# Turning the rows of the second part by transposing DMAs instead of by TensorE

## The chip, the cores and the metric

One core of a Trainium2 chip runs the whole program. The time is device time of one execution, in microseconds (us); before the change it is 3302.31 us, the median of three runs (3301.95 to 3308.06). Engines: PE is TensorE, DVE is VectorE, ACT is ScalarE, POOL is GpSimd, SP is SyncE, which here only issues DMAs. Each has its own instruction queue and works in order; a wait holds up all that stands behind it on that engine.

## The reference

Three steps, one after the other, on 8 x 3072 = 24576 rows of 256 numbers:

```python
X = fft(fft(x, axis=1), axis=2).real              # rows of 256
do = x @ w_skip > 0                               # only these rows meet an expert
e = argmax(x @ w_gate); g = softmax(x @ w_gate)[e]
x[do] += g * (relu(x @ w1[e]) @ w2[e])            # 8 experts, 256 -> 1024 -> 256
h = x @ w_in                                      # 256 -> 2048
P = a0 + a1*h + a2*h**2 + a3*h**3
Q = 1 + |b0|*|h| + |b1|*h**2
out = (P / (Q + 1e-6)) @ w_out                    # 2048 -> 256
```

## The kernel before, in words

Every float32 number is carried as two float16 numbers, a high half (the rounded value) and a low half (what is left), and every product is three float16 matmuls: high by high, high by low, low by high.

The first part (to about 566 us) does the Fourier transforms, decides the route of each row, and scatters rows of 258 numbers (256 values, row number, gate weight) into a sorted list XS in HBM. Rows without an expert come to lie in tiles of 512, rows with one in batches of 256 of one expert.

The second part, which the change touches, works on 48 tiles of 512 rows. 22 come from XS straight (tile `xt`), 26 are made by the experts (tile `xf`), each from two of 52 batches (tile `xm`). It is one loop over 48 x 8 = 384 iterations `i`, each of which takes 256 of the 2048 columns of `h` of a tile. In an iteration, in written order:

- `z_mm1(i)`: 12 matmuls of 512 columns give `u` in PSUM. PE needs the rows turned: 128 of their 256 values on the partitions, row numbers along the free axis.
- `z_1(i)`: ACT makes T (L968) and Y (L969) from `u`; DVE makes T (L970) from T and `u`. `u` has two PSUM buffers, which the experts' first product uses too.
- `z_3(i-1)` (L978, ACT), `z_mm2(i-5)` (24 matmuls into `accz`), and after the last piece of a tile `z_end`: a copy by ACT (L1016) and four scatters by POOL (L1017).
- `z_hi(i-2)`: DVE's L988, gh from T and Y, both in SBUF.
- one step or none of the experts' list `all_moe`: half the first product of a batch, with its evacuation (L923, L924), the begin of the next batch (`moe_begin`), the other half, half the second product, its other half with L932, which adds the expert's rows to `xm`.
- `z_2(i)` (L974) and `z_4(i-1)` (L982) on ACT; `z_lo(i-3)`, DVE's L1000; `z_rest(i-2)`, DVE's L993 and then POOL's L994, which reads T and V and writes V. L1000 reads that V one iteration later.
- where `i % 8` is 3, `begin` of the next tile, and where it is 5, `begin_2`: they make that tile's turned halves, which are read from the next `i % 8 == 0` on.

So on DVE the order around a tile's begin is L988, (expert work), L1000, L993, (begin), L970, L988. POOL's L994 follows L993.

Turning a piece of 256 rows, before: `transpose_half` (L872 to L878) puts four 128x128 float32 blocks through PE against an identity (L876) into one PSUM bank, ACT copies it as the high half (L877), DVE subtracts that from the PSUM bank for the low half (L878). A tile takes two such pieces, half a tile at `i % 8 == 3` and half at 5; a batch takes one.

SP issues in written order: the loads of `xt` (two buffers), of `xm` (three) and of the expert's weights `mw` (2 MB, two buffers, waits for PE to be done with the batch before last), and the loads and stores that split the later experts' weights (L1034 to L1050).

Of the kernel before, what the change touches and what calls it, by code (L numbers as in the profile page):

```python
# [8 lines left out]
F32 = mybir.dt.float32  # L9
F16 = mybir.dt.float16  # L10
I32 = mybir.dt.int32
AF = mybir.ActivationFunctionType
ALU = mybir.AluOpType
AX = mybir.AxisListType
PSUM = bass.MemoryType.PSUM
SYNC = mybir.DependencyInfo(mybir.DependencyClass.Sync, mybir.DependencyReason.DATA)

B, SEQ, D = 8, 3072, 256
# [5 lines left out]
TILE = 512  # L24
# [8 lines left out]
HALF = 256  # L33
# [95 lines left out]
def program(tc, x, w_skip, w_gate, w1, w2, w_in, w_out, a, b, f1, cs, tw, tok, ut, small, lt8, slot, out):  # L129
    nc = tc.nc  # L130
    pe, act, dve, pool, sp = nc.tensor, nc.scalar, nc.vector, nc.gpsimd, nc.sync
    es = ExitStack()
    with es:
# [7 lines left out]
        ident = pers.tile([128, 128], F32, name="ident")  # L141
# [122 lines left out]
        rows = {}  # L264
# [323 lines left out]
        for r in range(R0):  # L588
            sp.dma_start(out=XS[SKIP0 + r * TILE:SKIP0 + (r + 1) * TILE, :].rearrange("(p r) c -> p r c", p=128),
                         in_=dum[:, None, :].to_broadcast([128, 4, ROW]))  # L590
# [48 lines left out]
        def pool_of(name, bufs, space=None):  # L639
            return fb.enter_context(tc.tile_pool(name=name, bufs=bufs, reuse_waits="tile", **({} if space is None else {"space": space})))  # L640

        wk = pool_of("wk", 1)
        xtp = pool_of("xtp", 2)
        xsp = pool_of("xsp", 2)
        ggp = pool_of("ggp", 4)
        elp = pool_of("elp", 4)
        hhp = pool_of("hhp", 2)
        xmp = pool_of("xmp", 3)
        xfp = pool_of("xfp", 2)
        pl = pool_of("pl", 1)  # L650
        pll = pool_of("pll", 1)
# [1 line left out]
        wsp = pool_of("wsp", 2)  # L653
        psh = pool_of("psh", 2, PSUM)
        psz = pool_of("psz", 1, PSUM)
        psm = pool_of("psm", 1, PSUM)

        wi = wk.tile([128, 4, 2, 1024], F16, name="wi")
        wo = wk.tile([128, 4, 2, 1024], F16, name="wo")
# [204 lines left out]
                if e % 2:  # L864
                    yield

        def split_pair(tag, n):
            th = xsp.tile([128, 2, n], F16, tag=tag + "h", name="th")
            tl = xsp.tile([128, 2, n], F16, tag=tag + "l", name="tl")
            return th, tl  # L870

        def transpose_half(src, th, tl, tag="mt"):  # L872
            u = psm.tile([128, 2, HALF], F32, tag=tag, name="ut")
            for h in range(2):
                for r in range(2):
                    pe.transpose(u[:, h, r * 128:r * 128 + 128], src[:, r, h * 128:h * 128 + 128], ident[:])  # L876
            act.activation(th, u[:], AF.Copy)  # L877
            dve.tensor_tensor(out=tl, in0=u[:], in1=th, op=ALU.subtract)  # L878

        def mm1(u, w, f0, nf, xh, xl):  # L880
            for s in range(nf):
                n = 0
                for k in range(2):
                    wh, wl = w(k, 0, f0 + s), w(k, 1, f0 + s)
                    for sta, mv in ((wh, xh), (wh, xl), (wl, xh)):
                        pe.matmul(u[:, s, :], lhsT=sta, rhs=mv[:, k, :], start=(n == 0), stop=(n == 5))  # L886
                        n += 1

        def mm2(acc, w, f0, nf, hh, hl, first, last):
# [9 lines left out]
        xf_of = {}  # L899

        def moe_begin(t):
            xh, xl = split_pair("m", HALF)
            transpose_half(t, xh[:], xl[:], "m")
            return xh, xl

        def moe_steps(t, w, xh, xl, xf, ids, k):

# [39 lines left out]
        Z = {}  # L947
        outs = []

        def z_begin(src, ids, n, k):  # L950
            if k == 0:
                Z[n] = dict(x=split_pair("z", TILE), ids=ids, src=src)
            xh, xl = Z[n]["x"]
            c = slice(k * HALF, k * HALF + HALF)
            transpose_half(Z[n]["src"][:, 2 * k:2 * k + 2], xh[:, :, c], xl[:, :, c])

        def z_mm1(i):
            n, j = divmod(i, 8)
            u = psh.tile([128, 2, TILE], F32, tag="h", name="u")
            mm1(u, wif, 2 * j, 2, *Z[n]["x"])  # L960
            T = elp.tile([128, 1024], F32, tag="T", name="T")
            V = elp.tile([128, 1024], F32, tag="V", name="V")
            Y = elp.tile([128, 1024], F32, tag="Y", bufs=5, name="Y")
            U[i] = dict(u=u[:].rearrange("p s n -> p (s n)"), T=T[:], V=V[:], Y=Y[:])

        def z_1(i):
            d = U[i]
            act.activation(d["T"], d["u"], AF.Square, scale=A[0], bias=A[1])  # L968
            act.activation(d["Y"], d["u"], AF.Abs, scale=A[4])  # L969
            dve.scalar_tensor_tensor(out=d["T"], in0=d["T"], scalar=A[2], in1=d["u"], op0=ALU.add, op1=ALU.mult)  # L970

        def z_2(i):
            d = U[i]
            act.activation(d["V"], d["Y"], AF.Square, bias=A[5])  # L974

        def z_3(i):
            d = U[i]
            act.activation(d["Y"], d["V"], AF.Ln, bias=A[6])  # L978

# [142 lines left out]
        def begin(n):  # L1122
            if n and not ready and cur["s_used"] == S2:
                while not ready:
                    next(moe)
            if ready:
                src, ids = ready.pop(0)
            else:
                s = cur["s_used"]
                src = xt.pop(("S", s))  # L1130
                ids = new_ids()
                dve.tensor_copy(out=ids[:], in_=src[:, :, D])
                cur["s_used"] += 1
            z_begin(src, ids, n, 0)

        def begin_2(n):
            z_begin(None, None, n, 1)
            feed()

        begin(0)  # L1140
# [43 lines left out]
        with tc.For_i(0, rem, 1) as it:  # L1184
            xf = xfp.tile([128, 4, D], F32, tag="xf", name="xf")
            ids = new_ids()
            for k in range(2):
                t = xmp.tile([128, 2, ROW], F32, tag="xm", name="xm")
                r = sp.value_load(plan[0:1, bass.ds(it * 2 + (C_LROW + k), 1)], min_val=0, max_val=NROWS - HALF)
                e = sp.value_load(plan[0:1, bass.ds(it * 2 + (C_LEXP + k), 1)], min_val=0, max_val=E - 1)  # L1190
                sp.dma_start(out=t[:], in_=rows_of(r, HALF))
                sp.dma_start(out=mw[k][:], in_=WD[bass.ds(e, 1)].rearrange("o p k h n -> p (o k) h n"))
                for _ in moe_steps(t, mw[k], *moe_begin(t), xf, ids, k):
                    pass
            n = NTILES
            for k in range(2):
                z_begin(xf, ids, n, k)
            for i in range(n * 8, n * 8 + 8):
                z_mm1(i)
                d = U[i]  # L1200
                act.activation(d["T"], d["u"], AF.Identity, scale=A[11], bias=A[10])
                act.activation(d["V"], d["u"], AF.Square)
                act.activation(d["Y"], d["u"], AF.Abs, scale=A[12])
                dve.tensor_tensor(out=d["T"], in0=d["T"], in1=d["u"], op=ALU.mult)
                dve.scalar_tensor_tensor(out=d["T"], in0=d["T"], scalar=A[9], in1=d["u"], op0=ALU.add, op1=ALU.mult)
                dve.scalar_tensor_tensor(out=d["V"], in0=d["V"], scalar=A[13], in1=d["Y"], op0=ALU.mult, op1=ALU.add)
                act.activation(d["Y"], d["V"], AF.Ln, bias=A[14])
                z_4(i)
                z_hi(i, 8)
                z_rest(i, 14)  # L1210
                z_lo(i, 8)
                z_mm2(i)
            z_end(n, False, 15)
# [27 lines left out]
```

## Time and profile before

| | |
|---|---|
| median of three runs | 3302.31 us |
| the profiled execution: its own time, its span | 3295.73 us, 3293.7 us |
| granted TensorE clock, mean | 0.959 |
| PE busy, share of the span | 3034.3 us, 92% |
| DVE | 2818.9 us, 86% |
| ACT | 2525.9 us, 77% |
| POOL | 1406.6 us, 43% |
| chain that ended last | PE 61%, DVE 20%, ACT 7%, issue 5% |
| L994, POOL, V from T and V, 128x1024 | 384 times, 2381 ns |
| L988, DVE, gh from T and Y, 128x1024 | 384 times, 2060 ns |
| L1000 and L993, DVE, 128x1024 | 384 times each, 1272 and 1275 ns |

Times of an instruction run from its start to its end; PE's matmuls and DVE's operations overlap their neighbours by a little, so sums are made from start to start. The share of busy time counts an operation that has started and waits for a resource as busy.

### The profile page before, as it was taken

What the parts mean: (1) busy time and instruction counts of PE and PEld (TensorE: products, weight loads), DVE (VectorE), ACT (ScalarE), POOL (GpSimd) and SP (SyncE); (2) the same over time, 40 slices, a digit from 0 to 9 for tenths busy, and PEclk for the clock granted to TensorE, in tenths of its full rate; (3) what the DMA queues carried; (4) which work ended last, traced back from release to release, by engine and by line L of the source; (5) the groups of instructions that cost most, each with busy time, mean ns of one, the idle gap of its engine ahead of it and who ended that gap; (6) DMA issues with size and microseconds to landing.
All of it is one profiled execution on the core that took longest, in us unless ns stands there. A gap on an engine that the chain in (4) does not pass through costs nothing.

```text
span 3293.7 us, 57696 instructions
## 1 busy us (share of the span) xinstructions
PE 3034.3 (92%) x23586; PEld 2214.6 (67%) x23586; DVE 2818.9 (86%) x2929; ACT 2525.9 (77%) x2694; POOL 1406.6 (43%) x796
## 2 busy tenths in 40 slices
PE   6678656799989999999999999999999999999996
PEld 5556444477767777776777777777777777777764
DVE  5667544899999999998899988999989999899986
ACT  5556442688878888888888888888888888888884
POOL 0445442454434444443444344444444444444444
PEclk8889877899999999999999999999999999999998
DMA  8344443131111112111211110011002000100000
GB/s 204 126 126 141 129 129 143 69 99 45 64 63 33 52 62 71 39 43 60 73 40 43 62 38 25 24 49 42 21 11 78 20 20 20 61 28 20 7 14 14
DMA packets 75617, 198.09 MB, mean 60 GB/s; under 512 B 12243, under 2 KB 36180, under 8 KB 72404
## 3 DMA queue, kind: packets, MB, share of 16 engines
q1 hardware_dynamic: 54612, 135.42, 13.7%
q0 software_dynamic: 18432, 50.55, 4.3%
q10 hardware_dynamic: 2304, 8.39, 0.6%
q8 instruction: 186, 3.05, 0.4%
q14 instruction: 83, 0.68, 0.1%
HBM read 190.69 MB, written 77.05 MB: 81 GB/s over the span
## 4 chain that ended last, share of the span: by engine, by line
PE 61%; DVE 20%; ACT 7%; issue 5%; another core or an unknown queue 3%; DMA 3%; POOL 0%; ACTq 0%; SPq 0%; DVEq 0%; POOLq 0%
PE u L886 26%; PE accz L896 20%; PE acc L896 8%; DVE gh L988 6%; DVE T L970 4%; DVE V L993 3%; PE u L256 2%; DVE gl L1000 2%; DMA out<-ob,ids 1%; ACT Y L969 1%; PE ut L876 1%; ACT T L968 1%; DMA xt<-in_x 1%; PE u L241 1%
## 5 line engine op out<-in xcount | busy, mean ns | idle before, releaser
L994 POOL TENSOR_TENSOR V<-T,V 128x1024 f32<-128x1024 f32 x384 | 914.2, 2381 | 1428.5 <-DVE V L993 1331.5
L896 PE MATMUL accz<-wo,gh 128*128 128x256 f16 x6144 | 1034.8, 274 | 2.8 <-ACT ob L1016 2.8
L886 PE MATMUL u<-th,wi 128*128 128x512 f16 x3072 | 984.6, 382 | 39.8 <-DVE T L970 38.7
L896 PE MATMUL accz<-wo,gl 128*128 128x256 f16 x3072 | 840.9, 274 | 13.0 <-DVE gl L1000 10.7
L886 PEld LDWEIGHTS <-wi 128*128 128x128 f16 x4608 | 453.2, 98 | 515.5 <-issue 61.3
L988 DVE SCALAR_TENSOR_TENSOR gh<-T,co,Y 128x1024 f16<-128x1024 f32 x384 | 791.1, 2060 | 0.0
L896 PEld LDWEIGHTS <-gh 128*128 128x128 f16 x6144 | 603.7, 98 | 156.3 <-issue 3.9
L968 ACT ACTIVATE T<-u,co 128x1024 f32<-128x1024 f32 x384 | 462.8, 1205 | 289.3 <-PE u L886 257.7
L970 DVE SCALAR_TENSOR_TENSOR T<-T,co,u 128x1024 f32<-128x1024 f32 x384 | 488.9, 1273 | 129.8 <-ACT Y L969 123.4
L886 PE MATMUL u<-tl,wi 128*128 128x512 f16 x1536 | 586.6, 382 | 0.1
L1000 DVE SCALAR_TENSOR_TENSOR gl<-V,co,Y 128x1024 f16<-128x1024 f32 x384 | 488.6, 1272 | 41.6 <-POOL V L994 41.6
L993 DVE SCALAR_TENSOR_TENSOR V<-V,co,gh 128x1024 f32<-128x1024 f32 x384 | 489.6, 1275 | 0.0
L978 ACT ACTIVATE Y<-V,co 128x1024 f32<-128x1024 f32 x384 | 442.8, 1153 | 0.0
L974 ACT ACTIVATE V<-Y,co 128x1024 f32<-128x1024 f32 x384 | 440.7, 1148 | 0.5 <-DVE gl L1000 0.4
L969 ACT ACTIVATE Y<-u,co 128x1024 f32<-128x1024 f32 x384 | 427.4, 1113 | 0.0
L982 ACT ACTIVATE Y<-Y 128x1024 f32<-128x1024 f32 x384 | 404.6, 1054 | 0.0
L896 PEld LDWEIGHTS <-gl 128*128 128x128 f16 x3072 | 301.8, 98 | 52.0 <-DVE gl L1000 13.5
L886 PE MATMUL u<-th,mw 128*128 128x256 f16 x1664 | 292.7, 274 | 7.7 <-DVE T L970 5.2
L1017 POOL DMA_INDIRECT out<-ob,ids x192 | 245.8, 1280 | 77.2 <-issue 44.2
L896 PE MATMUL acc<-mw,hh 128*128 128x256 f16 x1664 | 278.1, 273 | 0.0
L886 PEld LDWEIGHTS <-mw 128*128 128x128 f16 x2496 | 245.8, 98 | 39.7 <-issue 9.8
L886 PE MATMUL u<-tl,mw 128*128 128x256 f16 x832 | 228.3, 274 | 1.3 <-DVE tl L878 1.3
(206 smaller groups left out, 3456.0 us busy)
## 6 DMA issues: line engine op xcount, KB each, us to landing
mw<-wd SPq DMA_DIRECT2D x50, 2048.0 KB
xt<-in_x SPq DMA_DIRECT2D x64, 384.0 KB
xm<-xs SPq DMA_DIRECT2D x52, 258.0 KB
wf<-in_moe_w SPq DMA_DIRECT2D x48, 256.0 KB
wd<-ws SPq DMA_DIRECT2D x48, 256.0 KB
xt<-xs SPq DMA_DIRECT2D x22, 516.0 KB
wd<-ws ACTq DMA_DIRECT2D x16, 512.0 KB
wr<-in_moe_w_in SPq DMA_DIRECT2D x4, 1024.0 KB
```

The source lines that it names most:

```text
L886: pe.matmul(u[:, s, :], lhsT=sta, rhs=mv[:, k, :], start=(n == 0), stop=(n == 5))
L896: pe.matmul(acc[:, r, :], lhsT=sta[:, c], rhs=mv, start=(first and r % 2 == 0 and s == 0 and n == 0), stop=(last and s == nf - 1 and n == ...
L968: act.activation(d["T"], d["u"], AF.Square, scale=A[0], bias=A[1])
L969: act.activation(d["Y"], d["u"], AF.Abs, scale=A[4])
L970: dve.scalar_tensor_tensor(out=d["T"], in0=d["T"], scalar=A[2], in1=d["u"], op0=ALU.add, op1=ALU.mult)
L974: act.activation(d["V"], d["Y"], AF.Square, bias=A[5])
L978: act.activation(d["Y"], d["V"], AF.Ln, bias=A[6])
L982: act.activation(d["Y"], d["Y"], AF.Exp, scale=-1.0)
L988: dve.scalar_tensor_tensor(out=h[:], in0=d["T"], scalar=A[a0], in1=d["Y"], op0=ALU.add, op1=ALU.mult)
L993: dve.scalar_tensor_tensor(out=d["V"], in0=d["V"], scalar=A[c], in1=h[:], op0=ALU.add, op1=ALU.mult)
L994: pool.tensor_tensor(out=d["V"], in0=d["T"], in1=d["V"], op=ALU.subtract)
L1000: dve.scalar_tensor_tensor(out=l[:], in0=d["V"], scalar=A[a0], in1=d["Y"], op0=ALU.add, op1=ALU.mult)
```

## The change

The rows are split before they are turned. ACT copies them as float16 (high half), DVE subtracts (low half), both into a tile `rows` in SBUF, and one transposing DMA, issued by SP, turns both halves, 16 blocks of 128x128 for a tile and 8 for a batch. A tile is now begun in one piece, at `i % 8 == 3`. PE's identity transposes and their PSUM bank go; the experts' second product gets two PSUM banks. The turned tile has another order, so a matmul's moving operand is four runs of 128 columns (two for a batch) where it was one of 512 (256). To make room, `xm` has two buffers for three and Y four for five.

```diff
+        rsp = pool_of("rsp", 1)
-        xmp = pool_of("xmp", 3)
+        xmp = pool_of("xmp", 2)
-        psm = pool_of("psm", 1, PSUM)
+        psm = pool_of("psm", 2, PSUM)
...
-        def transpose_half(src, th, tl, tag="mt"):
-            u = psm.tile([128, 2, HALF], F32, tag=tag, name="ut")
-            for h in range(2):
-                for r in range(2):
-                    pe.transpose(u[:, h, r * 128:r * 128 + 128], src[:, r, h * 128:h * 128 + 128], ident[:])
-            act.activation(th, u[:], AF.Copy)
-            dve.tensor_tensor(out=tl, in0=u[:], in1=th, op=ALU.subtract)
+        def split_turned(src, nr, tag):
+
+            rows = rsp.tile([128, 2, nr, D], F16, tag=tag, name="rows")
+            act.activation(rows[:, 0], src, AF.Copy)
+            dve.tensor_tensor(out=rows[:, 1], in0=src, in1=rows[:, 0], op=ALU.subtract)
+            t = xsp.tile([128, 2, nr, 2, 128], F16, tag=tag, name="turned")
+            sp.dma_start_transpose(out=t[:].rearrange("p l r h c -> p (l r h) c"), in_=rows[:].rearrange("p l r d -> p (l r d)"))
+            return t[:, 0], t[:, 1]
...
-                        pe.matmul(u[:, s, :], lhsT=sta, rhs=mv[:, k, :], start=(n == 0), stop=(n == 5))
+                        pe.matmul(u[:, s, :], lhsT=sta, rhs=mv[:, :, k, :], start=(n == 0), stop=(n == 5))
...
         def moe_begin(t):
-            xh, xl = split_pair("m", HALF)
-            transpose_half(t, xh[:], xl[:], "m")
-            return xh, xl
+            return split_turned(t[:, :, 0:D], 2, "m")
...
-        def z_begin(src, ids, n, k):
-            if k == 0:
-                Z[n] = dict(x=split_pair("z", TILE), ids=ids, src=src)
-            xh, xl = Z[n]["x"]
-            c = slice(k * HALF, k * HALF + HALF)
-            transpose_half(Z[n]["src"][:, 2 * k:2 * k + 2], xh[:, :, c], xl[:, :, c])
+        def z_begin(src, ids, n):
+            Z[n] = dict(x=split_turned(src[:, :, 0:D], 4, "z"), ids=ids)
...
-            Y = elp.tile([128, 1024], F32, tag="Y", bufs=5, name="Y")
+            Y = elp.tile([128, 1024], F32, tag="Y", name="Y")
...
-            z_begin(src, ids, n, 0)
+            z_begin(src, ids, n)
 
         def begin_2(n):
-            z_begin(None, None, n, 1)
             feed()
```

## Rows read from the trace of the kernel before

**Rows 1.** Busy time by stage: stretch, length, engines, granted clock, DMA share, GB/s.
```profile
566.00:620.00 54.00, 39.85 (x217) 23.11 (x218) 41.80 (x102) 36.82 (x41) 17.94 (x14) 0.82 0.31 108
...
1200.00:3000.00 1800.00, 1786.14 (x13268) 1302.79 (x13267) 1664.61 (x1368) 1514.56 (x1533) 776.59 (x388) 1.00 0.13 42
```

**Rows 2.** DVE's groups by line, 1200 to 3000: busy, mean ns, idle before, releaser.
```profile
L988 DVE SCALAR_TENSOR_TENSOR gh<-T,co,Y 128x1024 f16<-128x1024 f32 x260 | 541.5, 2083 | 0.0
...
L970 DVE SCALAR_TENSOR_TENSOR T<-T,co,u 128x1024 f32<-128x1024 f32 x260 | 331.2, 1274 | 93.0 <-ACT Y L969 88.0 <-issue 4.3
...
...
L878 DVE TENSOR_TENSOR tl<-ut,th 128x512 f16<-128x512 f32 x102 | 69.2, 678 | 0.4 <-ACT th L877 0.4
```

**Rows 3.** Timeline of PE around one group of transposes: start, length, instruction.
```profile
1515.22 0.60 PE L876 MATMUL ut<-ident,xf 128*128 128x128 f32 x4
1515.65 0.38 PE L886 MATMUL u<-th,wi 128*128 128x512 f16 x1
```

**Rows 4.** Tile ut: count, shortest, median and longest ns, first and last start.
```profile
L877 ACT ACTIVATE th<-ut x148: 582/597/627, 569.3 to 3191.2; 128x512 f16<-128x512 f32 x148
```

**Rows 5.** Timeline of DVE and POOL in the last tile.
```profile
3195.88 1.28 DVE L993 SCALAR_TENSOR_TENSOR V<-V,co,gh 128x1024 f32<-128x1024 f32 x1
...
3197.08 0.68 DVE L878 TENSOR_TENSOR tl<-ut,th 128x512 f16<-128x512 f32 x1
...
3198.87 1.89 DVE L988 SCALAR_TENSOR_TENSOR gh<-T,co,Y 128x1024 f16<-128x1024 f32 x1
...
3201.88 1.27 DVE L993 SCALAR_TENSOR_TENSOR V<-V,co,gh 128x1024 f32<-128x1024 f32 x1
...
3203.29 2.38 POOL L994 TENSOR_TENSOR V<-T,V 128x1024 f32<-128x1024 f32 x1 [3.62 <-DVE V L993]
...
3204.26 2.48 DVE L988 SCALAR_TENSOR_TENSOR gh<-T,co,Y 128x1024 f16<-128x1024 f32 x1
```

**Rows 6.** Timeline of the same two behind the last `z_1`.
```profile
3259.12 1.27 DVE L988 SCALAR_TENSOR_TENSOR gh<-T,co,Y 128x1024 f16<-128x1024 f32 x1
...
3259.35 3.25 POOL L994 TENSOR_TENSOR V<-T,V 128x1024 f32<-128x1024 f32 x1 [3.62 <-DVE V L993]
```

**Rows 7.** Timeline of the same two behind a tile's scatters.
```profile
1529.37 3.49 DVE L988 SCALAR_TENSOR_TENSOR gh<-T,co,Y 128x1024 f16<-128x1024 f32 x1
1529.38 2.38 POOL L994 TENSOR_TENSOR V<-T,V 128x1024 f32<-128x1024 f32 x1
```

**Rows 8.** SP's DMA queue on the page: packets, MB, share of 16 engines.
```profile
q1 hardware_dynamic: 54612, 135.42, 13.7%
```

**Rows 9.** Timeline from a tile's begin to its first matmul.
```profile
1020.60 1.28 DVE L970 SCALAR_TENSOR_TENSOR T<-T,co,u 128x1024 f32<-128x1024 f32 x1 [0.59 <-ACT Y L969]
...
1042.77 0.38 PE L886 MATMUL u<-th,wi 128*128 128x512 f16 x1
```

**Rows 10.** Timeline of the second part's start.
```profile
568.16 1.08 PE L876 MATMUL ut<-ident,xt 128*128 128x128 f32 x4
...
572.46 0.59 PE L886 MATMUL u<-th,wi 128*128 128x512 f16 x1 [0.69 <-ACT th L877]
...
591.30 0.27 PE L886 MATMUL u<-th,mw 128*128 128x256 f16 x1 [2.57 <-ACT th L877]
592.15 0.69 DVE L878 TENSOR_TENSOR tl<-ut,th 128x512 f16<-128x512 f32 x1
```

**Rows 11.** Timeline of PE in the first part, L241 and what follows it.
```profile
300.26 0.81 PE L241 MATMUL u<-o1h,nid 128*128 128x384 f16 x2
300.87 0.32 PE L256 MATMUL u<-f2t,o1h 128*128 128x276 f16 x1
```

**Rows 12.** Timeline of ACT and DVE where they are closest.
```profile
1511.34 1.11 ACT L969 ACTIVATE Y<-u,co 128x1024 f32<-128x1024 f32 x1
1511.46 1.28 DVE L993 SCALAR_TENSOR_TENSOR V<-V,co,gh 128x1024 f32<-128x1024 f32 x1
```

More of the change, by code (lines that the diff above doesn't have):

```diff
@@ L865, in fill @@
                     yield
[L867 to L870, printed above, removed]
-        def transpose_half(src, th, tl, tag="mt"):
-            u = psm.tile([128, 2, HALF], F32, tag=tag, name="ut")
-            for h in range(2):
-                for r in range(2):
-                    pe.transpose(u[:, h, r * 128:r * 128 + 128], src[:, r, h * 128:h * 128 + 128], ident[:])
-            act.activation(th, u[:], AF.Copy)
-            dve.tensor_tensor(out=tl, in0=u[:], in1=th, op=ALU.subtract)
+        def split_turned(src, nr, tag):
[5 more added lines that the diff above has]
+            return t[:, 0], t[:, 1]
         def mm1(u, w, f0, nf, xh, xl):
@@ L1195, in program @@
             n = NTILES
-            for k in range(2):
-                z_begin(xf, ids, n, k)
+            z_begin(xf, ids, n)
             for i in range(n * 8, n * 8 + 8):
```

## The prediction

> **What bounds the kernel now.** The change touches the second part only, so I read the stages first. In the window from 1200 to 3000 us TensorE (PE) is busy 1786 of 1800 us at a granted clock of 1.00, its upper level of 2.4 GHz, VectorE (DVE) 1665 and ScalarE 1515; while the second part starts, from 566 to 620, PE is busy 40 of 54 us [rows 1]. That looks like a stage bound by PE alone. The groups by line put a doubt on it: L988 takes 2.08 us in the mean, twice its neighbours, and L970 has 93 us of idle time ahead of it [rows 2]. The timeline says what L988's length is made of. In the last tile, where no expert work lies between, L988 starts at 3204.26 while GpSimd (POOL) is in L994, from 3203.29 to 3205.67, and ends 1.07 us after that: 2.48 us. Where a half split (L878) stood between L993 and L970, L988 took 1.89 [rows 5]. Alone it takes 1.27 [rows 6]. So L988 waits until POOL is done, and whatever time passes between L993 and L988 shortens this wait by as much.
>
> The Trainium skill (SBUF — State Buffer, section "SBUF: two separate sides") has a rule for it: VectorE with two SBUF inputs and a GpSimd operation share a port pair, and the one that starts first holds it for its whole instruction. The trace agrees both ways: 2.48 us for L988 behind L994, and 3.25 us for L994 where L988 had started 0.23 us earlier.
>
> From this follows how much room DVE has. It is idle 135 of the 1800 us. Were it never idle ahead of L970, the 260 L988 would take 2.48 instead of 2.08, 103 us more. Less 38 us, since in the 65 places with a half split of a tile (two in eight iterations) they take 0.59 less; and 33 us more, since once per tile, 32 times, L994 comes late behind four scatters and L988 takes 3.49, 1.0 more than 2.48, which the mean already holds and the 2.48 doesn't [rows 2, 5, 7]. So 98 of the 135 us would come back as waiting for POOL and 37 are real room, 2.1%. In the stretch from 620 to 3160 us, 2540 us, that is 52 us. The chain L993, L994, L988 is a second bound hardly behind PE.
>
> **Removed from PE.** One group of four transposes takes from 1515.22 to 1515.65, 0.43 us, far less than four durations [rows 3]; there are 148 groups [rows 4], so 64 us, and 102 x 0.43 = 44 us in the window of 1800 [rows 2]. By PE alone that is the gain.
>
> **The split.** ScalarE copies 2 x 512 columns of a tile before and 1024 after: at most twice 0.60 us [rows 4], and it has 16% idle [rows 1]; no cost. For an expert batch DVE's subtract keeps its 512 columns and its place behind L988, when POOL is done: no change (0 to the wait of 1.2 us if POOL is at work, x 52 = 62 us at most; I take 0). For a tile two subtracts of 0.60 us become one of 1024 columns, and its second input stops being in PSUM: now both are in SBUF. By the nearest row, 1.27 us for L988 alone, it takes 1.2 from start to start. It stands right behind L993 and ahead of the next L970. The old halves there cost the chain nothing: L993 at 3195.88 to L988's end at 3200.76 is 4.88 us with a half between, 3201.88 to 3206.74 is 4.86 without [rows 5]. The new one starts 1.20 after L993, L994 at 1.41, 0.21 later, which is the case of the rows where L994 took 3.25 us [rows 6]. So POOL ends 0.87 us later, L988 too: 48 x 0.87 = 42 us on the chain. Ends: 0, if DVE was idle there anyway; and 2.4, if POOL starts first: then the split ends 3.78 + 1.07, L970 takes 1.2, L988 1.27, 7.3 in place of 4.9. I take 0.87, since DVE waited for ScalarE's copy ahead of 102 subtracts for 0.4 us in all [rows 2].
>
> **The transfer.** It is not in the trace. A tile is 0.52 MB in 2048 pieces of 256 bytes. From below by SP's queue, 135.42 MB in 13.7% of 16 x 3293.7 us, 300 KB a us: 1.7 us. From above, if each piece takes as long as a mean packet there, 0.132 us, on 16 engines: 16.9 us [rows 8]. I take the middle of the two in ratio, 5.4 us, and 2.7 for an expert batch. The cover is the way from L970 behind the split, 1020.60, to the first matmul of the next tile, 1042.77: 22.2 us, the median of 47 tiles [rows 9]. A batch is begun four steps of its own list ahead of use, longer still. So the transfer is hidden even at the upper end; without the cover it would be 48 x 5.4 = 259 us. On SP's queue it stands behind loads and stores that wait for PE and DVE work that is earlier in the written order, so it isn't held up by more than one 2 MB load, 7 us at the rate above.
>
> The Trainium skill (VectorE: DVE Perf Modes, section "The three transpose paths") gives 1309 ns for a 128x128 transpose by DMA against 390 on TensorE and advises TensorE where PSUM will do. By it a tile would take 16 x 1.3 = 21 us, an estimate, one behind another. No run here shows it yet; it is the third rival's rule.
>
> **The start.** Two places have no cover. Tile 0: PE transposed at 568.16 and its matmuls began at 572.46 [rows 10]. Now copy (1.2), subtract (1.2) and transfer (1.7 to 16.9) follow each other: 572.3 to 587.5, with 5.4 us 576.0, 3.5 later. Expert batch 0: its matmuls began at 591.30, and DVE got to its subtract at 592.15; now the transfer (0.9 to 8.5) comes behind: 593.7 to 601.3, I take 595.5, 4.2 later. Sum 8 us, between 2 and 25.
>
> **The rest.** One Y buffer fewer: L969 must wait for the L1000 of four iterations before. At 1511.34 it started just before that was over, and L993 stood at 1511.46 [rows 12]: the push of some 0.1 us ends with L993, and lies ahead of L988, where the wait for POOL swallows it. Third xm buffer gone: the load now waits for L932 of the batch before, and has a whole matmul step before it is read. Second PSUM buffer, earlier release of xt: nothing waited there. The matmuls now read runs of 128 columns, 3 more starts in each of 4608 and 1 in each of 2496. Bounds: 0, and the L241 with its 96 runs, 0.305 us from start to start or 3.2 ns a run [rows 11], 44 + 8 = 52 us of PE time; there the output is in pieces too, and runs are of 8 bytes against 256, so I take 0.
>
> **Sum.** PE's 64 us can't come out, since the chain has 52 to give. With PE faster I let three quarters of it be given, -39; the chain grows by 42; the start by 8: +11 us on the profiled run's own 3295.7, so 3306.7. The median of the three runs lies 6.6 higher, so 3313.
>
> **Rivals.** (1) PE was the bound and its time comes out. For it: 99.2% busy, and a DVE that is idle 7.5%. Against: the lengths of L988. Then -52 + 8 and the split at no price: 3258, or 3280 with half of its price. (2) POOL goes first at every tile's split, because ScalarE's copy comes late: 48 x 2.4 = 115 in place of 42, 3386. It decides where the copy ends over 0.2 us behind L993. For it: ScalarE may be held up by the Y buffer; against: those 0.4 us. (3) The transfer outlasts its cover: each us beyond 22 costs 48; at 30 us 384, 3690. By the page's 21 us a free queue would still hide it, one with a 2 MB load ahead would not. Against: the share of DMA is 0.13 in the window [rows 1]. (4) The change doesn't take the load off PE: reading in runs costs the 52 us. Then PE gives 12, some of the chain's price is hidden, and 3318 comes out.
>
> **Chances.** My forecast 0.52, with its own range 3294 (all 52 given, start 2) to 3345; rival 1 0.25, rival 2 0.08, rival 3 0.08, rival 4 0.07. Three runs of this kernel tell about 0.2% from no change, 6.6 us. Faster: nearly all of rival 1 and a tenth of the forecast, 0.28; same: a quarter of the forecast, some of rivals 1 and 4, 0.19; slower: the rest, 0.53. The range 3258 to 3375 leaves out half of rival 1's lower side, most of rival 2 and rival 3.
>
> **What would show it.** Right: L994 behind the splits at 3.2 us instead of 2.37; PE's share in the window down from 99% to some 97.5 with waits for L970; DVE with no idle over 5%; the first tile's matmuls 2 to 15 us after 572.5. Wrong: PE still at 99% and the window's work done in 44 us less (rival 1); subtracts of 2.5 to 3.6 us (rival 2); first matmuls of a tile that wait for the transfer (rival 3); longer times from start to start of L886 (rival 4).

## The result, and the profile after

The changed kernel took 3329.16 us (median of 6 runs, 3313.35 to 3334.48) against 3301.42 us (6 runs, 3291.25 to 3308.06): 1.008 times as long, with a 95% interval of 1.0057 to 1.0104. By the medians that is 28 us slower, by the ratio 26; the forecast was 3313 us, slower by 11, in a range of 3258 to 3375. Measured once more on a second chip it took 1.0051 times the time of the kernel before [1.0032, 1.0071]: 17 us by the ratio, 21 between the medians, because its seven runs fall into two groups, 3307 to 3312 and 3322 to 3325 us.

Line numbers moved. What was L970, L988, L1000, L993, L994, L969 is now L961 (T), L979 (gh), L991 (gl), L984 (V on DVE), L985 (V on POOL), L960 (Y on ACT); the matmuls are L883 and L893, the split is L871 (ScalarE) and L872 (VectorE), the transfer L874.

The page of the kernel after, busy time of the engines and GpSimd's group:

```profile
PE 2996.8 (90%) x22994; PEld 2155.0 (65%) x22994; DVE 2874.2 (86%) x2881; ACT 2541.4 (76%) x2646; POOL 1459.0 (44%) x796
...
L985 POOL TENSOR_TENSOR V<-T,V 128x1024 f32<-128x1024 f32 x384 | 958.2, 2495 | 1416.3 <-DVE V L984 1319.2
```

The two stages of [rows 1], after:

```profile
566.00:620.00 54.00, 27.15 (x135) 13.97 (x135) 27.18 (x78) 23.81 (x28) 15.98 (x15) 0.65 0.36 120
1200.00:3000.00 1800.00, 1741.53 (x12739) 1249.49 (x12737) 1681.56 (x1323) 1513.86 (x1491) 808.86 (x386) 0.99 0.20 57
```

The groups of [rows 2], after:

```profile
L979 DVE SCALAR_TENSOR_TENSOR gh<-T,co,Y 128x1024 f16<-128x1024 f32 x258 | 561.3, 2176 | 0.0
L961 DVE SCALAR_TENSOR_TENSOR T<-T,co,u 128x1024 f32<-128x1024 f32 x258 | 330.2, 1280 | 73.8 <-ACT Y L960 72.2 <-issue 1.1
```

TensorE, busy 1786 of 1800 us before, is busy 1742: the transposes are gone, and yet 258 instead of 260 steps (iterations of the loop) fit into the window. What it lost in work it waits for. The next rows are TensorE's waits from 560 to 3200 us (total, times, longest); the wait for DVE's T is a matmul that can't have its bank of PSUM back, the memory that TensorE writes to:

```profile
PE u L883 <- DVE T L961: 94.5, 54, 7.1
PE u L883 <- DMA turned<-rows: 13.9, 2, 7.1
```

Before, the same wait for T came to 43.9 us in 25 times. On the chain that ended last PE's share fell from 61% to 37% and DVE's rose from 20% to 33%: TensorE now waits for DVE and GpSimd. GpSimd's L985 is busy 958 us in all at 2.50 us in the mean; one takes 2.38 when undisturbed [rows 5]. 52 of its 384 instances take over 2.9 us, 4 did before.

**Where the time went.** DVE runs T once in each of the 384 steps, so its T of step 10 and of step 368 are two marks in the timeline, in both kernels. Before:

```profile
660.56 1.27 DVE L970 SCALAR_TENSOR_TENSOR T<-T,co,u 128x1024 f32<-128x1024 f32 x1
...
3158.33 1.28 DVE L970 SCALAR_TENSOR_TENSOR T<-T,co,u 128x1024 f32<-128x1024 f32 x1 [2.07 <-ACT Y L969]
```

After:

```profile
677.21 1.28 DVE L961 SCALAR_TENSOR_TENSOR T<-T,co,u 128x1024 f32<-128x1024 f32 x1
...
3198.92 1.28 DVE L961 SCALAR_TENSOR_TENSOR T<-T,co,u 128x1024 f32<-128x1024 f32 x1 [1.19 <-ACT Y L960]
```

The stretch between them, 2497.8 us before, is 2521.7 after, 23.9 longer, and 2515.9, 18.1 longer, in the profile on the second chip. The first mark lies 16.6 us later, but 14.5 of this arose ahead of the change: the first part's last copy (L311) started at 568.13 before and at 582.67 here, in code that is the same in both. So I compare kernels by the stretch and by the ratio of their timed runs, not by the spans of their profiles. The stretch comes from one profile each; the two of the changed kernel are 5.8 us apart, and smaller differences of stretches show nothing by themselves.

### The profile page after: what moved, and what is told of

It reads as the page before. It is cut to its first block, busy times and chain, and to the rows that moved or that the text cites. A ratio compares the mean times of both kernels' runs of the same rounds, so it can differ in the third digit from the quotient of the medians.

```text
span 3332.7 us, 56415 instructions
## 1 busy us (share of the span) xinstructions
PE 2996.8 (90%) x22994; PEld 2155.0 (65%) x22994; DVE 2874.2 (86%) x2881; ACT 2541.4 (76%) x2646; POOL 1459.0 (44%) x796
## 4 chain that ended last, share of the span: by engine, by line
PE 37%; DVE 33%; issue 11%; ACT 9%; DMA 3%; another core or an unknown queue 3%; POOL 2%; SPq 0%; DVEq 0%; ACTq 0%; POOLq 0%
PE u L883 15%; DVE gh L979 12%; PE accz L893 11%; DVE V L984 6%; PE acc L893 6%; DVE T L961 5%; DVE gl L991 4%; PE u L256 3%; DMA out<-ob,ids 2%; ACT Y L960 2%; ACT T L959 2%; POOL out L1008 1%; ACT V L965 1%; PE u L241 1%
## 5 line engine op out<-in xcount | busy, mean ns | idle before, releaser
L985 POOL TENSOR_TENSOR V<-T,V 128x1024 f32<-128x1024 f32 x384 | 958.2, 2495 | 1416.3 <-DVE V L984 1319.2
L883 PE MATMUL u<-turned,wi 128*128 128x512 f16 x4608 | 1083.9, 386 | 99.0 <-DVE T L961 90.6
L893 PE MATMUL accz<-wo,gh 128*128 128x256 f16 x6144 | 1032.4, 273 | 11.6 <-ACT ob L1007 11.6
L893 PE MATMUL accz<-wo,gl 128*128 128x256 f16 x3072 | 839.6, 273 | 14.1 <-DVE gl L991 11.9
L883 PEld LDWEIGHTS <-wi 128*128 128x128 f16 x4608 | 456.6, 99 | 591.8 <-issue 143.8
L979 DVE SCALAR_TENSOR_TENSOR gh<-T,co,Y 128x1024 f16<-128x1024 f32 x384 | 831.6, 2166 | 0.0
L893 PEld LDWEIGHTS <-gh 128*128 128x128 f16 x6144 | 603.1, 98 | 167.6 <-issue 18.8
L961 DVE SCALAR_TENSOR_TENSOR T<-T,co,u 128x1024 f32<-128x1024 f32 x384 | 491.3, 1280 | 111.4 <-ACT Y L960 108.8
L960 ACT ACTIVATE Y<-u,co 128x1024 f32<-128x1024 f32 x384 | 426.6, 1111 | 145.7 <-DVE gl L991 142.8
L991 DVE SCALAR_TENSOR_TENSOR gl<-V,co,Y 128x1024 f16<-128x1024 f32 x384 | 488.8, 1273 | 48.7 <-POOL V L985 48.7
L984 DVE SCALAR_TENSOR_TENSOR V<-V,co,gh 128x1024 f32<-128x1024 f32 x384 | 489.8, 1275 | 0.0
L969 ACT ACTIVATE Y<-V,co 128x1024 f32<-128x1024 f32 x384 | 438.7, 1142 | 0.0
L893 PEld LDWEIGHTS <-gl 128*128 128x128 f16 x3072 | 301.4, 98 | 53.0 <-DVE gl L991 14.9
L883 PE MATMUL u<-turned,mw 128*128 128x256 f16 x2496 | 294.5, 275 | 11.0 <-DMA turned<-rows 7.1
L893 PE MATMUL acc<-mw,hh 128*128 128x256 f16 x1664 | 278.1, 273 | 0.0
L883 PEld LDWEIGHTS <-mw 128*128 128x128 f16 x2496 | 246.5, 99 | 42.2 <-issue 11.7
L261 DVE SCALAR_TENSOR_TENSOR o2l<-u,o2h 128x552 f16<-128x552 f32 x96 | 69.9, 728 | 186.8 <-ACT o2h L260 173.8
L893 PE MATMUL acc<-mw,hl 128*128 128x256 f16 x832 | 226.8, 273 | 0.0
```

The costliest lines, as they stand in the source:

```text
L883: pe.matmul(u[:, s, :], lhsT=sta, rhs=mv[:, :, k, :], start=(n == 0), stop=(n == 5))
L893: pe.matmul(acc[:, r, :], lhsT=sta[:, c], rhs=mv, start=(first and r % 2 == 0 and s == 0 and n == 0), stop=(last and s == nf - 1 and n == ...
L979: dve.scalar_tensor_tensor(out=h[:], in0=d["T"], scalar=A[a0], in1=d["Y"], op0=ALU.add, op1=ALU.mult)
L984: dve.scalar_tensor_tensor(out=d["V"], in0=d["V"], scalar=A[c], in1=h[:], op0=ALU.add, op1=ALU.mult)
L985: pool.tensor_tensor(out=d["V"], in0=d["T"], in1=d["V"], op=ALU.subtract)
L991: dve.scalar_tensor_tensor(out=l[:], in0=d["V"], scalar=A[a0], in1=d["Y"], op0=ALU.add, op1=ALU.mult)
```

## The experiments

My theory after the result: the tile's split, the L872 of 1024 columns, pushes GpSimd's L985 by 0.9 us once per tile (the push, from here on), and that costs some 40 us; TensorE's 64 us are worth some 10. Rivals: the fourth Y buffer; VectorE's time for the split, whatever its operands; the batches' half of the change.

**1. TensorE's transposes alone.** The kernel before, in which the four transposes are issued for the first group only and the two splitting operations read that PSUM tile every time:

```diff
-            u = psm.tile([128, 2, HALF], F32, tag=tag, name="ut")
-            for h in range(2):
+            if "ut" not in fixed:
+                fixed["ut"] = psf.tile([128, 2, HALF], F32, tag="ut", name="ut")
+            u = fixed["ut"]
+            for h in range(2 if not used else 0):
                 for r in range(2):
                     pe.transpose(u[:, h, r * 128:r * 128 + 128], src[:, r, h * 128:h * 128 + 128], ident[:])
+            used.append(1)
```

> The kernel before, with PE's transposes left out: four are done once into a fixed PSUM bank, and ACT and DVE read that bank at every split, so the rows are not turned; all else, DVE's and ACT's splits included, stays. It takes 64 us from PE and adds nothing. Theory (the chain L993, L994, L988 of DVE and POOL is a second bound with about 52 us of room, of which the changed kernel gave some 20): 20 to 45 us faster than before, 3256 to 3281, PE's share from 1200 to 3000 us down to some 97 to 98%. Rival (PE alone is the bound): 64 us faster, 3237 within 6.

3159.45 against 3168.92 us, 0.9963 [0.9951, 0.9976]; the stretch is 2491.1 us, 6.7 shorter. In a window of 1800 us of it:

```profile
1075.00:2875.00 1800.00, 1755.74 (x12895) 1263.26 (x12894) 1676.90 (x1369) 1519.45 (x1538) 783.18 (x389) 1.00 0.13 42
```

TensorE has 44 us of idle time where it had 14, and DVE's busy time hardly moved (1677 us, 1665 before). Taking away 147 of the 148 groups (some 63 us of TensorE) is worth 7 us of the stretch, 9 between the medians, 12 by the ratio: 7 to 12 us, below the 20 to 45 expected. That is the real room, and the prediction had counted on 39.

**2. The tile's subtraction alone.** The changed kernel without the L872 of the tiles, the first one excepted; ScalarE's copy, the transfer and the batches stay:

```diff
-            dve.tensor_tensor(out=rows[:, 1], in0=src, in1=rows[:, 0], op=ALU.subtract)
+            if nr == 2 or len(Z) == 0 and not rows_z[1:]:
+                dve.tensor_tensor(out=rows[:, 1], in0=src, in1=rows[:, 0], op=ALU.subtract)
```

> The changed kernel without DVE's subtract for the tiles: the low half of the tile's rows is made once and then kept, only ACT writes the high half; the batches keep theirs. Theory (the subtract delays POOL's L994 by 0.87 us and so L988, 48 times): 43 us faster than the changed kernel, 3278 to 3294, POOL's V from T and V back at 2.37 us in the mean. Rival (the fourth Y buffer, for which ACT waited 143 us, is what costs): at most 10 us faster, 3319 to 3330.

3156.27 against 3168.92 us, 0.9966 [0.9955, 0.9978]; stretch 2485.5, 30 to 36 us shorter than with the subtraction (on other chips; 43 were expected). The loss hangs on this one instruction, as the theory said. It doesn't tell yet whether by the push or by VectorE's own 1.21 us.

**3. The high half read from PSUM, two pieces.** ScalarE copies the high half into a PSUM bank as well, and DVE subtracts that, in two pieces of 512 columns at the steps 3 and 4 of a tile:

```diff
+            u = psm.tile([128, 2, D], F32, tag="ph", bufs=1, name="ph")
+            act.activation(u[:], z["rows"][:, 0, c], AF.Copy)
+            dve.tensor_tensor(out=z["rows"][:, 1, c], in0=z["src"][:, c, 0:D], in1=u[:], op=ALU.subtract)
```

> The changed kernel with the tile's subtract in two pieces of 512 columns, at i % 8 of 3 and 4, and with the high half read from PSUM: ACT copies it there from the rows' float16 half (two copies of 512 columns more per tile), and the experts' second product has one PSUM bank again. DVE keeps all of its 1.2 us per tile, but one input only is in SBUF. Theory (two SBUF inputs hold POOL up): POOL's V from T and V is 2.37 us behind the splits too, the pieces pass in the time in which L988 would wait, 35 to 43 us faster than the changed kernel, 3284 to 3296, faster than the kernel before. Rival (it is DVE's time for 1024 columns that costs): as the changed kernel, 3322 to 3338, since DVE's time is the same and ACT has 50 us more.

3187.92 against 3168.92 us, 1.0057 [1.0044, 1.007]; stretch 2515.8. A miss: GpSimd's operation was back at 2.38 us in the mean, and nearly nothing was gained. The piece at step 4 stands in the step in which a tile's result is copied out and scattered, and the waits of GpSimd's scatters for that copy came to 42 us, where they are 4 in the changed kernel. But run 7, with no piece at step 4, has 39 us of them, so this reason isn't shown. Two copies of ScalarE were added and the subtraction was cut in two: it isn't a clean test of the push. Runs 7, 8 and 10 move the pieces; run 9 tests the operand alone.

**4. The fifth Y buffer given back** (one ob buffer less and the second xf elsewhere, to make room):

```diff
-            Y = elp.tile([128, 1024], F32, tag="Y", name="Y")
+            Y = elp.tile([128, 1024], F32, tag="Y", bufs=5, name="Y")
```

> The changed kernel with five Y buffers, as before the change; the output tile of a tile of rows has one buffer for two and the second xf lies elsewhere to make room. ACT's waits for a Y buffer (143 us in the trace of the changed kernel) go. Theory (the wait ends ahead of L988, which waits for POOL anyway): up to 8 us faster than the changed kernel, 3321 to 3331. Rival (the buffer is what keeps the room from being used): 15 to 25 us faster, 3304 to 3314.

3187.85 against 3168.92 us, 1.006 [1.0047, 1.0073]; stretch 2513.4. Not the Y buffer, at most a small part of it (12 sizes it in the kernel before).

**5. The changed kernel on another chip,** for its profile beside the next ones.

> The changed kernel itself once more, beside the kernel before on the chip on which its parts are run, so that its profile can be laid against theirs. On the first chip it took 1.008 times the time of the kernel before. Theory (the loss lies in the second part: the tile's split pushes GpSimd's operation 48 times by 0.9 us, 42 us, less some 10 us that TensorE's transposes are worth, and some 8 us more for the fourth Y buffer): about 1.008 again, +22 to +30 us, and the stretch from the T operation of step 10 to that of step 368 about 24 us longer than in the kernel before. Rival (part of the loss is the slower first part of the one profiled execution, 14.5 us): 1.003 to 1.005, +10 to +15 us.

3322.14 against 3301.49 us, 1.0051 [1.0032, 1.0071]; stretch 2515.9. That is 17 us by the ratio, below the 22 to 30 of the theory, and the ratio alone would nearly fit the rival too. The stretch doesn't: 18.1 us lie in the steps 10 to 368, so the loss isn't the first part's.

**6. Only the batches changed,** tiles as before, five Y buffers:

```diff
         def moe_begin(t):
-            xh, xl = split_pair("m", HALF)
-            transpose_half(t, xh[:], xl[:], "m")
-            return xh, xl
+            return split_turned(t[:, :, 0:D], 2, "m")
```

> Only the batches of 256 rows are split row by row and turned by the transposing DMA; the tiles of 512 rows are turned by TensorE and split from PSUM as before, with five Y buffers. Theory (the tile's split from two SBUF operands is what costs): the loss is gone and TensorE is rid of 100 of its 148 groups of transposes, so 0.997 to 1.001 of the kernel before (-10 to +3 us). Rival (the batches' splits and transfers cost as much as the tiles'): 1.003 to 1.006 (+10 to +20 us).

3300.61 against 3301.49 us, 1.0003 [0.9992, 1.0014]; stretch 2497.3. No loss and no gain, with 52 of the 148 groups of transposes off TensorE (not 100, as the expectation has it: the tiles keep two each).

**7. The PSUM pieces at steps 3 and 5,** where the kernel before had its two evictions:

```diff
-            if ZB <= i % 8 < ZB + PIECES and i // 8 + 1 < NTILES:
-                split_piece(Z[i // 8 + 1], i % 8 - ZB, PIECES)
+            if i % 8 in (ZB, ZB + 2) and i // 8 + 1 < NTILES:
+                split_piece(Z[i // 8 + 1], (i % 8 - ZB) // 2, PIECES)
```

> The changed kernel with the tile's subtraction in two pieces of 512 columns, whose high half ScalarE copies into PSUM first, at the steps 3 and 5 of a tile, where the kernel before has its two evictions, instead of the steps 3 and 4 of the run with the high half in PSUM, where ScalarE's copy stood beside the tile's last copy. Theory of the push: GpSimd's operation takes 2.37 us behind both pieces, and now nothing else stands in the way, so 0.996 to 0.999 of the kernel before (-4 to -12 us). Rival (not the push but VectorE's and ScalarE's time and the place of the pieces): as the run with the pieces at 3 and 4, 1.004 to 1.007 (+13 to +22 us).

3326.35 against 3301.49 us, 1.0075 [1.0058, 1.0092]; stretch 2516.3. A second miss, for a reason of its own. TensorE's waits in it, 700 to 3160 us:

```profile
PE u L893 <- DVE T L973: 60.6, 42, 7.1
PE u L893 <- DMA turned<-rows: 18.3, 7, 6.6
PE accz L903 <- ACT ob L1019: 13.3, 12, 2.0
```

The transfer now leaves two steps later, and the next tile's matmuls wait for it, up to 6.6 us; the step from T 7 to T 8 of a tile took 7.13 us in the mean instead of 6.84, over 44 tiles 13 us of the 18.5 by which the stretch is longer than before. The other 6 aren't assigned. This is the prediction's third rival, at a place where it was really to be had.

**8. The same with five Y buffers.**

> The same pieces at the steps 3 and 5, and the fifth Y buffer given back (one ob buffer less). Theory: another 0 to 8 us below the run with the pieces at 3 and 5, 0.994 to 0.998 of the kernel before, which would beat both kernels. Rival (pieces cost as they did at 3 and 4): 1.001 to 1.005.

3320.31 against 3301.49 us, 1.0061 [1.0045, 1.0077]; stretch 2513.5. A third miss: the transfer is late here too, up to 7.5 us.

**9. One SBUF operand fewer.** The tile's subtraction takes 1024 columns at the same place, but its second operand is a constant in PSUM, so that the low half isn't made (for the constant's bank the experts' sums have one PSUM buffer instead of two, as in the runs with pieces):

```diff
-            dve.tensor_tensor(out=rows[:, 1], in0=src, in1=rows[:, 0], op=ALU.subtract)
+            if nr == 4:
+                if not fixed:
+                    fixed.append(psm.tile([128, 1, 2 * D], F32, tag="ph", bufs=1, name="ph"))
+                    dve.memset(fixed[0][:], 0.0)
+                dve.tensor_tensor(out=rows[:, 1].rearrange("p (a r) d -> p a r d", a=2), in0=src.rearrange("p (a r) d -> p a r d", a=2), in1=fixed[0][:].rearrange("p a (r d) -> p a r d", r=2).to_broadcast([128, 2, 2, D]), op=ALU.subtract)
+            else:
+                dve.tensor_tensor(out=rows[:, 1], in0=src, in1=rows[:, 0], op=ALU.subtract)
```

> The changed kernel, but VectorE subtracts from the tile's rows a constant that lies in PSUM instead of the high half in SBUF (the low half is left out of the result by that): the same 1024 columns at the same place, with one SBUF operand fewer and no other operation added or moved. Theory of the push (GpSimd's operation behind the split takes 3.25 us only because of the two SBUF operands): 2.37 us behind it, and the run without the tile's subtraction is repeated: 0.995 to 0.998 of the kernel before. Rival (it is the 1.2 us of VectorE's own time, whatever its operands): GpSimd's operation is short and the time still stays near the changed kernel's, 1.003 to 1.008.

3300.18 against 3305.01 us, 0.999 [0.9981, 1.0]; stretch 2496.4, 19.5 us shorter than that of run 5. GpSimd's operation in it, 700 to 3160 us, and then in run 5:

```profile
L993 POOL TENSOR_TENSOR V<-T,V 128x1024 f32<-128x1024 f32 x354 | 844.1, 2384 | 1337.2 <-DVE V L992 1252.4 <-DVE ids L1131 83.5 <-issue 1.0
```
```profile
L985 POOL TENSOR_TENSOR V<-T,V 128x1024 f32<-128x1024 f32 x351 | 875.2, 2493 | 1315.7 <-DVE V L984 1233.3 <-DVE ids L1123 82.0
```

This is the clean test. The subtraction takes 1.21 us in both, only the push is gone, and with it the loss. That it no longer waits for ScalarE's copy doesn't matter: in run 5 this wait is 0.2 us over all 48 tiles. A ratio of 0.999 lies just above the 0.995 to 0.998 of the theory, so the push is worth some 20 us, not 40: 0.61% between the ratios of run 5 and run 9, on two chips, is 20 us. Run 11 has the push, though its batches are turned by TensorE, and ran beside run 9: it took 20.4 us longer (12.2 us of stretch). The step from run 9 to run 2, 11 us of stretch on another chip, goes with VectorE's own 1.21 us times 44 tiles: of 53 us of work a fifth would count.

One tile shows where the other half of the push goes. Run 5, the changed kernel (start, duration, instruction; first DVE, then POOL):

```profile
2711.70 1.21 DVE L872 TENSOR_TENSOR rows<-xf,rows 128x1024 f16<-128x1024 f32 x1
...
2714.40 1.82 DVE L979 SCALAR_TENSOR_TENSOR gh<-T,co,Y 128x1024 f16<-128x1024 f32 x1
2716.14 1.27 DVE L991 SCALAR_TENSOR_TENSOR gl<-V,co,Y 128x1024 f16<-128x1024 f32 x1
...
2719.32 1.28 DVE L961 SCALAR_TENSOR_TENSOR T<-T,co,u 128x1024 f32<-128x1024 f32 x1 [0.67 <-ACT Y L960]
...
2725.53 1.27 DVE L991 SCALAR_TENSOR_TENSOR gl<-V,co,Y 128x1024 f16<-128x1024 f32 x1
...
2711.92 3.22 POOL L985 TENSOR_TENSOR V<-T,V 128x1024 f32<-128x1024 f32 x1 [4.40 <-DVE V L984]
2715.49 1.60 POOL L1008 DMA_INDIRECT out<-ob,ids  x1 [0.35 <-ACT ob L1007]
...
2720.93 2.38 POOL L985 TENSOR_TENSOR V<-T,V 128x1024 f32<-128x1024 f32 x1
```

The same tile in run 9, 15.32 us earlier on the clock:

```profile
2696.38 1.21 DVE L878 TENSOR_TENSOR rows<-xf,ph 128x1024 f16<-128x1024 f32 x1
...
2699.04 1.28 DVE L987 SCALAR_TENSOR_TENSOR gh<-T,co,Y 128x1024 f16<-128x1024 f32 x1
2700.24 1.28 DVE L999 SCALAR_TENSOR_TENSOR gl<-V,co,Y 128x1024 f16<-128x1024 f32 x1
...
2703.97 1.28 DVE L969 SCALAR_TENSOR_TENSOR T<-T,co,u 128x1024 f32<-128x1024 f32 x1 [1.22 <-issue]
...
2709.64 1.27 DVE L999 SCALAR_TENSOR_TENSOR gl<-V,co,Y 128x1024 f16<-128x1024 f32 x1
...
2696.59 2.37 POOL L993 TENSOR_TENSOR V<-T,V 128x1024 f32<-128x1024 f32 x1 [4.40 <-DVE V L992]
2700.13 1.06 POOL L1016 DMA_INDIRECT out<-ob,ids  x1 [1.16 <-ACT ob L1015]
...
2705.04 2.38 POOL L993 TENSOR_TENSOR V<-T,V 128x1024 f32<-128x1024 f32 x1
```

Both splits start 0.21 to 0.22 us ahead of GpSimd's operation (0.14 to 0.23 in 47 of the 48 tiles of each), which takes 3.22 us beside the one and 2.37 beside the other. Put the two splits on one instant (take 15.32 from the first kernel's times): gl comes 0.58 us later with the push, but the next T only 0.03 later, because DVE stood idle ahead of it anyway, 1.22 us without the push and 0.67 with it. On GpSimd nearly all of it is absorbed too, at first: the first of its four scatters starts 0.04 us later, since it waits 0.35 us for ScalarE's copy, where it waited 1.16. But this scatter takes 1.60 us for 1.06 (in the mean of all tiles 1.73 for 1.46; why was not studied), and GpSimd's next operation and the gl behind it are 0.57 late. Over 44 tiles GpSimd's operation ends 0.88 us later, the first scatter starts 0.51 later, the next operation 0.73 and the one after it 0.45. On DVE the same difference, each tile's T of step 3 set to zero, is 0.70 us at gl, 0.32 at the T behind it and 0.41 four steps after the split, where it stays: half of 0.87.

**10. Pieces at steps 2 and 3, PSUM, five Y buffers:** a version that computes everything and has neither the push nor the late transfer nor a piece at step 4.

The pieces are those of run 3, one step earlier:

```diff
-        ZB = 3
+        ZB = 2
+        PIECES = 2
```

> The two pieces with the high half in PSUM at the steps 2 and 3 of a tile, so that neither stands in the step of the tile's last copy (4) and the transfer leaves as early as in the changed kernel, and five Y buffers. The step from T operation 7 to 8, which took 0.3 us longer with pieces at 3 and 5 where TensorE waited for the transfer, should be back at 6.84 us. Theory of the push: 0.995 to 0.999 of the kernel before, the best of these kernels. Rival (VectorE's own time): 1.002 to 1.006.

3308.98 against 3305.01 us, 1.0009 [1.0, 1.0018]; stretch 2497.8, the kernel before to a tenth. Step 7 to 8 is back at 6.89 us. Against run 4, on another chip, which differs in the pieces and their operand, 15.6 us of stretch are gone. It doesn't beat the kernel before. Where TensorE's 7 to 12 us go in it, to ScalarE's extra copies or to the start, was not tested. No version here beats both, except by leaving work out.

**11. Only the tiles changed,** batches by TensorE from PSUM, four Y buffers:

```diff
         def moe_begin(t):
-            return split_turned(t[:, :, 0:D], 2, "m")
+            xh = xsp.tile([128, 2, HALF], F16, tag="mh", name="th")
+            xl = xsp.tile([128, 2, HALF], F16, tag="ml", name="tl")
+            transpose_half(t, xh[:], xl[:], "m")
+            return xh, xl
```

> The other half of the change alone: tiles split row by row and turned by the transposing DMA, batches by TensorE and from PSUM as before, four Y buffers. Theory (the tiles' split carries the whole loss): 1.004 to 1.009 of the kernel before, as the changed kernel. Rival (the loss needs the batches' splits as well, whose two SBUF operands stand beside GpSimd's operation too): 0.999 to 1.003.

3320.61 against 3305.01 us, 1.0048 [1.0036, 1.006]; stretch 2508.6, with 52 long operations of GpSimd as in the changed kernel. The tiles carry the loss. Whether the batches add the 7 us of stretch to run 5 stays open: the ratios (1.0048, 1.0051) don't tell the two kernels apart.

**12. The kernel before with four Y buffers.**

```diff
-            Y = elp.tile([128, 1024], F32, tag="Y", bufs=5, name="Y")
+            Y = elp.tile([128, 1024], F32, tag="Y", name="Y")
```

> The kernel before with four Y buffers instead of five and nothing else changed, to size this one term alone. The prediction's step (a fourth buffer only moves a wait in front of an operation that waits for GpSimd anyway): 0.9995 to 1.0005 of the kernel before, under 2 us, the stretch from the T operation of step 10 to that of step 368 within 3 us of 2497.8. Rival (the run that gave the changed kernel its fifth buffer back was up to 8 us shorter over that stretch): 1.001 to 1.0025 (+3 to +8 us).

3166.68 against 3169.03 us, 0.9992 [0.9983, 1.0001]; stretch 2498.3. The fourth buffer costs nothing, in the kernel before, although ScalarE's Y there waits 91 us in all, in 132 places, for the gl that gives the buffer back.

## Why the prediction was right, and where its sum was not

The sign and the mechanism of the push held. The sum is another matter: two of its terms were too large, TensorE's relief by 27 to 32 us and the push by some 22, and they are of opposite sign. That 11 us came out as near as it did to the 17 and 26 measured is in part luck.

- **Room, the failed step.** The prediction found 52 us of room in the chain from L993 to L988 and let TensorE's relief use 39 of it. Run 1 measured 7 to 12. The step took the idle time ahead of T as room, after subtracting what comes back as waiting for GpSimd, and let a faster TensorE use three quarters of it. The waits of the kernel before (700 to 3160 us) and of run 1 (572 to 3032, the same steps) show why it doesn't (total, times, longest):

```profile
ACT T L968 <- PE u L886: 231.6, 116, 6.6
DVE T L970 <- ACT Y L969: 113.4, 137, 3.0
PE u L886 <- DVE T L970: 28.4, 20, 5.3
```
```profile
ACT T L974 <- PE u L892: 241.3, 125, 8.6
DVE T L976 <- ACT Y L975: 108.2, 128, 3.4
PE u L892 <- DVE T L976: 69.8, 50, 7.1
```

  DVE's T waits for ScalarE's Y, ScalarE's T for TensorE's u, and TensorE for DVE's T, which gives the bank back. With less work TensorE waits 41 us more for T, and DVE's wait for Y is 5 us shorter. That these three waits form a ring which a lighter TensorE can't shorten is read from the rows; no run tests it. In the changed kernel DVE's idle time in the window went from 135 to 118 us only; the sign "no idle over 5%" didn't come (it is 6.6%).
- **The tile's split.** 0.87 us in 48 tiles, 42 us: as a length on GpSimd it came out, 958 us in L985 against 914 before, 44 more. As a price it was some 20 us (run 9 against run 5: 20 by the ratios, 19.5 of stretch), since half of it falls into waits that were there anyway: DVE's ahead of the next T, and the scatters' for ScalarE's copy (23.5 us from 700 to 3160 us in run 9, 4.2 in run 5).
- **The rule on the shared port,** first the rows: with both operands in SBUF and a start 0.22 us ahead, GpSimd's operation ends 0.85 us later than with one of them in PSUM, 3.22 against 2.37 us, beside a subtraction of the same length. When GpSimd's operation started, the subtraction had 0.99 us to run. It is the operand, not VectorE's work as such. The Trainium skill (SBUF — State Buffer, section "SBUF: two separate sides") says that the shared port pair goes to whichever starts first, for its whole instruction, a VectorE operation with two SBUF inputs or a GpSimd operation that reads SBUF; the trace agrees, with 0.85 of the 0.99 us.
- **The transfer.** 5.4 us estimated, 3.9 measured at the start, where it isn't covered (3.89 to 3.96 in six profiles). First part's last copy, split, transfer and first matmul of tile 0, after:

```profile
582.67 0.40 ACT L311 ACTIVATE ev<-u 128x276 f32<-128x276 f32 x1 [1.75 <-issue]
...
583.13 1.06 ACT L871 ACTIVATE rows<-xt 128x1024 f16<-128x1024 f32 x1
...
584.22 1.23 DVE L872 TENSOR_TENSOR rows<-xt,rows 128x1024 f16<-128x1024 f32 x1 [0.20 <-ACT rows L871]
...
585.47 1.74 SPq L874 DMA_TRANSPOSE turned<-rows  x1
...
589.39 1.01 PE L883 MATMUL u<-turned,wi 128*128 128x512 f16 x2 [6.80 <-DMA turned<-rows]
```

  From 585.47 to 589.39, 3.92 us. By the 1309 ns that the Trainium skill has for a block (VectorE: DVE Perf Modes, section "The three transpose paths") 16 blocks one behind another would be 21 us, an estimate; the measurement decides, at 0.25 us a block in one instruction. Under its 22 us of cover the transfer never made TensorE wait in the changed kernel's steady stretch (both of its waits are at the start); two steps later, in run 7, it did.
- **The start.** From the last L311 to the first matmul 6.72 us, 4.33 before (568.13 to 572.46): 2.4 later for tile 0, where 3.5 were forecast. On the clock the first matmul comes 16.9 us after 572.5, beyond the 2 to 15 of the sign, but 14.5 of them are the first part's. Batch 0's first matmul waited 7.1 us for its transfer, where it had waited 2.6 for the split, but the T of step 10 came only 0.5 us later against that of step 0. From the last L311 to the T of step 10 it is 92.4 us before, 94.5 after and 95.2 in run 5: 2 to 3 us, at the lower end of 2 to 25, where 8 were taken.
- **At nothing:** the Y buffer (run 12; the prediction had its wait too short, at 0.1 us, and its price right), the matmuls' reading in runs of 128 columns (a 512-column matmul lasts 379 ns in the median, as the 0.38 of [rows 3]). The batches: no price in run 6, and of their 52 subtractions one took 2.85 us in the changed kernel, the others 0.67 to 0.68. ScalarE's larger copies for the tiles were in no run by themselves.
- **The other signs.** L985 behind the splits at 3.2 us, as said; TensorE's share of the window 96.8% with waits for T, where 97.5% was said.
- **The rivals.** TensorE as the bound fell with run 1. GpSimd first at the splits didn't occur, subtracts took 1.21 to 1.23 us. Late transfers are real, but need a later issue. Reading in runs cost nothing.

The terms as measured are -7 to -12 (TensorE), +20 (push) and 2 to 3 (start), 10 to 16 in sum, against 17 and 26 us by the ratios of the two comparisons. The rest, from 1 to 16 us, isn't assigned; VectorE's single operation in place of two that GpSimd hardly saw, and the batches, are candidates, and neither was shown. Run 9, which has every term but the push, came to -3 us by its ratio; 0.41 us in each of 48 tiles, the delay that stays in the comparison by tiles, brings that to the 17 us of run 5. The 9 us more on the first chip stay open.

## What to carry to other kernels

Before moving an operation's input from PSUM to SBUF, look at what GpSimd starts within its duration: here the delay lay on GpSimd's operation (3.22 us for 2.37), not on the one that was changed. Then follow the delay to the next wait of the engine behind it: if that wait is for a third engine, part of the delay is free, as half of it was here, and the length read off GpSimd overstates the price. And the work of an engine that is busy 99% of the time need not be worth its length (63 us gave 7 to 12); cut it out in a run of its own and see what the end does.

## What the runs showed of the hardware that was not expected

- A DMA that turns 0.52 MB of float16 within SBUF took 3.9 us from issue to the first matmul that reads it, 1.74 of them on the issuing queue (the median of the 100 issues, 48 of this size and 52 of half of it, is 1.41 us, the longest 9.1).
- The first part, the same code in every kernel here, ended about 14 us apart in two profiles (568 and 583 us) and some 130 us earlier in runs 1 to 4 and 12 (438 to 442 us), beside which the kernel before took 3169 us. The chip's number doesn't decide it: run 12 and runs 9 to 11, where the kernel before took 3305 us, have the same one on record. The stretch of steps 10 to 368 hardly noticed: 2498.3 us in run 12, 2497.8 in the kernel before, which has one Y buffer more. Why the first part differs was not studied.
